# Recurrent attention with two expert mixtures: the old state added on TensorE, and y taken to rows and logits in f32

## The chip, the core and the metric

The kernel runs on one core of a Trainium2 chip. The metric is the device time of one execution in microseconds (us). Engines: PE is TensorE, DVE is VectorE, ACT is ScalarE, POOL is GpSimd, SP issues most of the DMAs.

## The reference, cut to what matters

Four batches of eight heads, 768 steps, head width 48. A recurrence makes y; its rows, 384 wide, go through two mixtures of eight experts, each row to one expert at most in each mixture.

```python
for t in range(S):
    state = alpha[:, :, t, :, None] * state + np.einsum('bhd,bhe->bhde', k[:, :, t], v[:, :, t])
    y[:, :, t] = np.einsum('bhd,bhde->bhe', q[:, :, t], state)
x = y.transpose(0, 2, 1, 3).reshape(B * S, H * D)
do_compute = x @ w_skip > 0                  # first mixture: other rows pass unchanged
e_idx = np.argmax(xc @ w_gate, axis=1)       # xc = x[do_compute]
y[mask] = gate_w[mask, None] * (np.maximum(xc[mask] @ w1[e], 0.0) @ w2[e])
...                                          # second mixture: all rows, its own gate and weights
```

## The kernel before, in words

**Attention by chunks.** The 768 steps of a batch are six chunks of 128, so there are 24 chunks (g) in all, c = 0 to 5 within a batch. Eight heads are four pairs, two heads of a pair on partitions 0 to 63 and 64 to 127. `prep` (L506) scans alpha's products over the chunk on DVE (L511, L515) and multiplies them into k and q, on GpSimd for most chunks (L519, L520). `emit_a` (L524) makes the scores (`ap`, L531), masks one half of the heads on DVE (L539) and the other on ACT and GpSimd (L536, L537), and transposes the keys (`kp`, L546). `emit_y` (L551) makes y in PSUM from the scores and from the old state (`yp`, L563 to L568). ACT writes 64 times y as f16 (`yh`, L571) and DVE the remainder as f16 (`yl`, L591). It then makes the chunk's own part of the state (`sp`, L578, L579); DVE adds the old state (L583) and multiplies by the chunk's whole decay (L585; L587 in the first chunk of a batch, which has no old state). `emit_r` (L602), one chunk late, turns y into rows and, in the same products, into the logits of both gates: the operand holds a selection of the pair's columns and the weights, in f16 halves (`rh`), so there are two products per pair, with `yh` (L612) and with `yl` (L613). ACT copies the rows out (L614), DVE sums the logits over the pairs and halves (L615).

**Order.** The order on every engine is the order of the code; nothing is reordered. An iteration g of the loop (L717) issues `emit_a(g+1)`, `prep(g+3)`, `emit_y(g)`, `emit_r(g-1)`. Between them `rt` puts short steps of the routing (`softmax_pick`, `rank`, `index`, `order`), which are mostly on DVE, some on PE (L284, L347); three chunks are one group of the routing. From g = 6 on, every second iteration splits a quarter of the first expert's weights into halves (`split_w`, L172: ACT, then GpSimd or DVE, L180).

**PSUM.** Banks have tags. `kp` and both `rp` (the rows' products) of a chunk share tag K with two banks, in turn; so the transposes of a chunk's keys wait until an earlier chunk's logits have been summed (L615). `ap`, `yp` and `sp` share tag B with four banks.

**Behind the attention.** The first mixture's tiles (gathered rows) and then the second's run as long rows of f16 products on PE, with weights streamed in by SP. They wait at their start for the last rows and lists of the routing.

Of the kernel before, what the change touches and what calls it, by code (L numbers as in the profile page):

```python
# [20 lines left out]
C = 128  # L21
# [9 lines left out]
# Each mixture's experts in the order of work: expert 0 first, in two parts (the second part's rows come from the last  # L31
# rows to be routed), then the others by falling length of their lists.
# [17 lines left out]
# further steps of routing in a chunk's time  # L50
RT = [1, 1, 1, 1, 1, 1, 1, 1, 1, 1, 1, 1, 1, 1, 1, 1, 0, 2, 0, 2, 10, 10, 7, 14]
# where the second mixture's first tiles are turned
TURNS2 = ((0, 3), (1, 1), (1, 5), (2, 1))
REL3 = (2, 1, 3, 3, 3, 3, 3, 1, 1)
# the chunks from which on GpSimd masks all scores
MASKP = 22
# steps of routing, and the ticks that a turn on TensorE waits, in the first mixture's parts
# [10 lines left out]
# in the second mixture's first part and in the others: where the weights are split, and the next part's tiles turned  # L68
SPLITS2 = (((2, 0), (2, 2), (2, 4), (2, 6)), ((0, 3), (0, 6), (1, 3), (1, 6)))
TURNS = (((2, 1), (2, 3), (2, 5)), ((0, 1), (1, 1), (2, 1), (2, 4)))  # L70
# quarters of an expert's weights whose lower halves GpSimd makes
# [35 lines left out]
def body(tc, qka, vN, rw, wg2, wg17, w1a, w2a, w1b, w2b, cst, zr, out, stop=9, dbg=None):  # L107
# [3 lines left out]
    with ctx:  # L111
# [15 lines left out]
        # sums of the logits in halves of the heads, scaled by SX twice  # L127
        lg = const.tile([128, 2, NB, 17], F32, name="lg")
        # selection of a head pair's rows, and the upper and lower halves of the scaled weights for the logits
        rh = const.tile([YP, NP, 130], F16, name="rh")  # L130
        wg2s = const.tile([128, 3, 8], F32, name="wg2s")
        # identity, and the halves of the second gate's scaled weights
# [5 lines left out]
        with ExitStack() as fctx, tc.manual_schedule():  # L138
# [6 lines left out]
            def bank(tag, name, *shape, parts=128, bufs=2):  # L145
                """a bank of PSUM, its front as [parts, *shape]"""
                t = ps.tile([128, 512], F32, tag=tag, name=name, bufs=4 if tag == "B" else bufs)
                v = t[0:parts, 0:int(np.prod(shape))]
                if len(shape) == 2:
                    v = v.rearrange("p (a b) -> p a b", a=shape[0])  # L150
                elif len(shape) == 3:
                    v = v.rearrange("p (a b c) -> p a b c", a=shape[0], b=shape[1])
                return v
# [41 lines left out]
            # Its short dependent steps are generators: 0 is yielded after each, 1 before TensorE's turn, 2 while it  # L195
            # waits for another, and the phases spread them between their own instructions.
# [31 lines left out]
            def finish(*which):  # L228
                """runs the given generators to their ends"""
                while any(r in active for r in which):  # L230
                    release()
                    rt()

            def softmax_pick(l, n, w, res, scale=1.0):
                """l: [128, n, w, 8]; gives the first maximum's one-hot and the exponentials of the scaled logits"""
# [29 lines left out]
            # running counts of the lists' entries in each partition  # L265
# [7 lines left out]
            def hold():  # L273
                """the bank of the short products, for one generator at a time, and TensorE's turn"""
# [5 lines left out]
            def rank(n, nl, ohm, before, res):  # L280
                """places of the rows in their lists, after those counted in before"""
# [11 lines left out]
            def wait(what, i):  # L293
                """until as many groups of rows are counted or indexed"""
# [9 lines left out]
            def numbered(n, nl, ohm, b0):  # L304
                """the one-hots times the two parts of the rows' numbers, 8 * blk + (partition + 1)"""
# [5 lines left out]
            def index(i, n, nl, ohm, on, rk, cols, region, first, last):  # L311
                """adds the rows' numbers to idx_ps at their places"""
# [48 lines left out]
            def order(i, counts):  # L361
                """the lists by falling length, the first list first: one-hot places of the lists [place, list]; each
                list's room; the order of the weights"""
# [33 lines left out]
            def ordered(i, src, t, dst):  # L397
                """dst [128, 7, t]: the index columns of the lists but the first in their order"""
# [14 lines left out]
            def to_lhs(x, hi, lo, m, tag="K"):  # L413
                """x: [m, 384] rows -> hi, lo: [128, 3, m]"""
# [6 lines left out]
            def ffn1(x, n, nf, xs, hs, each):  # L421
                """relu(x @ w1) as two halves hs: [128, 8, n]"""
# [16 lines left out]
            def ffn2(x, yp, hs, c, each):  # L439
                """h @ w2 for the rows c of h"""  # L440
# [7 lines left out]
            def ffn2t(x, c0, c1, hs, yps, each):  # L448
                """(h @ w2) transposed for the rows c0 to c1 of h: yps of [128, rows], in thirds of the columns"""
# [19 lines left out]
            def turn1(j, t):  # L469
                """a tile's rows as the columns of a product's operand"""  # L470
# [35 lines left out]
            def prep(g, parts):  # L506
                """products of alpha over the chunk's prefixes into q, their inverses into k"""
# [16 lines left out]
            def emit_a(g):  # L524
                """decayed scores of a chunk, keys by queries, masked; the keys transposed"""
# [25 lines left out]
            def emit_y(g):  # L551
                """y of a chunk from its scores and the state; the state's step"""
# [3 lines left out]
                yh, yl = st["ys", g] = [wk.tile([YP, NP, C], F16, tag=f"y{h}", name=f"y{h}") for h in "hl"]  # L556
                # the last chunk's in two banks, each read while the other is filled
                n = 2 if g == NB - 1 else NP
                for p0 in range(0, NP, n):
# [11 lines left out]
                    A.activation(out=yh[:, p0:p0 + n], in_=yp, func=AF.Copy, scale=SX)  # L571
                    if n < NP:
                        V.scalar_tensor_tensor(out=yl[:, p0:p0 + n], in0=yp, scalar=SX, in1=yh[:, p0:p0 + n], op0=ALU.mult, op1=ALU.subtract)
                if c < NC - 1:
                    ks = st.pop(("ks", g))
                    sp = bank("B", "sp", NP, D)
                    for p in range(NP):
                        T.matmul(sp[0:64, p, :], lhsT=ks[:, p, 0:64], rhs=v[:, p, 0:48], start=True, stop=True)  # L578
                        T.matmul(sp[64:128, p, :], lhsT=ks[:, p, 64:128], rhs=v[:, p, 48:96], start=True, stop=True)  # L579
                    sn = wk.tile([GP, NP, D], F32, tag="s", name="s")  # L580
                    e = pt.pop(g)[:, :, C:C + 1].to_broadcast([GP, NP, D])
                    if c:
                        V.tensor_tensor(sn, st.pop(("s", g)), sp, op=ALU.add)  # L583
                        rt()
                        V.tensor_tensor(sn, sn, e, op=ALU.mult)  # L585
                    else:
                        V.tensor_tensor(sn, sp, e, op=ALU.mult)  # L587
                    st["s", g + 1] = sn
                    rt()
                if n == NP:  # L590
                    V.scalar_tensor_tensor(out=yl, in0=yp, scalar=SX, in1=yh, op0=ALU.mult, op1=ALU.subtract)  # L591
                else:
                    release()
# [8 lines left out]
            def emit_r(g):  # L602
                """rows of x and their logits of both gates"""
# [3 lines left out]
                yh, yl = st.pop(("ys", g))  # L607
                for i2 in range(2):
                    rp = bank("B" if g == NB - 1 else "K", "rp", 2, 130)
                    for p in range(2):  # L610
                        q = 2 * i2 + p
                        T.matmul(rp[:, p, :], lhsT=yh[:, q, :], rhs=rh[:, q, :], start=True, stop=False)  # L612
                        T.matmul(rp[:, p, 0:113], lhsT=yl[:, q, :], rhs=rh[:, q, 0:113], start=False, stop=True)  # L613
# [581 lines left out]
```

## Time and profile before

| | us |
|---|---|
| median of 3 runs | 627.39 (622.05 to 632.94) |
| profiled execution, span from first to last instruction | 635.2 |
| PE busy | 538.6 (85%) |
| DVE busy | 430.5 (68%) |
| ACT busy | 252.5 (40%) |
| POOL busy | 315.5 (50%) |

The profile gives the span of its execution and no other time for it. A busy share is a mean over stages: the first 200 us are the attention, the rest the mixtures. "Idle before" names what ended an engine's wait. The chain of waits is followed back from the last instruction, at each step to what released it or to the instruction before it on its engine. The granted clock is a share of TensorE's full speed. A product in f32 shows as two records on PE.

### The profile page before, as it was taken

How to read it: one execution, taken by the hardware profiler on the slowest of the kernel's cores; microseconds unless marked ns; L12 is line 12 of the kernel's file. 1: busy time of each engine (PE TensorE's matmuls, PEld its weight loads, DVE VectorE, ACT ScalarE, POOL GpSimd, SP SyncE). 2: the span in 40 equal slices, each digit the busy share in tenths (PEclk: the TensorE clock that was granted, in tenths of full speed). 3: DMA queues.
4: the chain of work that ended last, by engine and by line, in shares of the span. 5: the costliest groups of instructions: out<-in, count | busy, mean ns of one | idle time of the engine just before them, and what ended most of it. 6: DMA issues, size and time to landing. Idle time of an engine off the chain costs nothing.

```text
span 635.2 us, 12933 instructions
## 1 busy us (share of the span) xinstructions
PE 538.6 (85%) x5089; PEld 385.7 (61%) x5089; DVE 430.5 (68%) x1123; ACT 252.5 (40%) x483; POOL 315.5 (50%) x269
## 2 busy tenths in 40 slices
PE   7898687697699779998868897979797989898994
PEld 4665454464467668888757866636364656564662
DVE  7988998989969788989889892381251626252530
ACT  2232332333334345555435623443353535443430
POOL 2453534434524575666655507366355555655501
PEclk7696996968869999999879998989898999998998
DMA  9561760653313765766665318435253344362001
GB/s 313 179 245 57 269 225 18 211 170 120 114 53 97 244 193 191 244 210 195 219 184 191 103 43 284 152 90 199 103 158 124 119 159 152 124 199 75 33 2 35
DMA packets 41464, 96.81 MB, mean 152 GB/s; under 512 B 3638, under 2 KB 28468, under 8 KB 41398
## 3 DMA queue, kind: packets, MB, share of 16 engines
q1 hardware_dynamic: 36662, 82.40, 38.9%
q0 software_dynamic: 4736, 13.53, 6.9%
q8 instruction: 42, 0.69, 0.5%
q14 instruction: 24, 0.20, 0.1%
HBM read 83.43 MB, written 12.99 MB: 152 GB/s over the span
## 4 chain that ended last, share of the span: by engine, by line
PE 48%; DVE 34%; issue 9%; another core or an unknown queue 3%; ACT 3%; DMA 2%; POOL 0%; POOLq 0%; DVEq 0%; ACTq 0%; SPq 0%
PE hp L431 6%; PE hp L432 6%; PE hp L430 6%; PE yp L443 4%; PE yp L444 4%; PE yp L445 4%; PE yp L567 3%; DVE pp L511 3%; DVE qka L515 3%; PE yp L563 2%; DVE s L585 2%; PE tp L417 2%; DVE hl L436 1%; DVE yl L591 1%
## 5 line engine op out<-in xcount | busy, mean ns | idle before, releaser
L436 DVE SCALAR_TENSOR_TENSOR h2l<-hp,h2h 128x352 f16<-128x352 f32 (+8 forms) x66 | 38.3, 586 | 105.4 <-ACT h2h L435 104.0
L180 POOL TENSOR_TENSOR w1l<-raw,w1h 128x768 bf16<-128x768 f32 x47 | 76.6, 1649 | 56.2 <-ACT w1h L178 56.0
L180 POOL TENSOR_TENSOR w0l<-raw,w0h 128x768 bf16<-128x768 f32 x47 | 77.3, 1651 | 45.9 <-ACT w0h L178 45.6
L519 POOL TENSOR_TENSOR qka<-qka 128x512 f32<-128x512 f32 (+1 forms) x24 | 27.5, 1147 | 91.1 <-DVE qka L515 72.0
L431 PE MATMUL hp<-x2l,w0h 128*128 128x352 f16 (+8 forms) x216 | 70.6, 331 | 1.4 <-DVE x2l L419 1.4
L430 PE MATMUL hp<-x2h,w0h 128*128 128x352 f16 (+8 forms) x216 | 71.0, 333 | 0.0
L432 PE MATMUL hp<-x2h,w0l 128*128 128x352 f16 (+8 forms) x216 | 70.5, 331 | 0.0
L443 PE MATMUL yp<-w1h,h2h 128*128 128x384 f16 (+1 forms) x192 | 63.2, 329 | 3.8 <-DVE h2l L436 3.8
L956 POOL DMA_INDIRECT out<-o,ixo x31 | 31.5, 1017 | 66.4 <-ACT o L1032 46.9
L431 PE MATMUL hp<-xl,w0h 128*128 128x200 f16 (+7 forms) x216 | 55.6, 265 | 10.4 <-DVE xl L419 10.2
L444 PE MATMUL yp<-w1l,h2h 128*128 128x384 bf16 (+1 forms) x192 | 63.2, 329 | 0.0
L445 PE MATMUL yp<-w1h,h2l 128*128 128x384 f16 (+1 forms) x192 | 63.1, 329 | 0.0
L432 PEld LDWEIGHTS <-w0l 128*128 128x128 bf16 x432 | 44.2, 102 | 29.3 <-POOL w1l L180 10.8
L455 PE MATMUL yp<-hl,w1h 128*128 128x200 f16 (+7 forms) x216 | 52.6, 252 | 3.9 <-DVE hl L436 3.9
L430 PE MATMUL hp<-xh,w0h 128*128 128x200 f16 (+7 forms) x216 | 55.8, 266 | 0.2 <-ACT xh L418 0.2
L432 PE MATMUL hp<-xh,w0l 128*128 128x200 f16 (+7 forms) x216 | 55.7, 266 | 0.0
L178 ACT ACTIVATE w0h<-raw 128x768 f16<-128x768 f32 x64 | 53.4, 836 | 3.7 <-DMA raw<-in_w1a 2.2
L454 PE MATMUL yp<-hh,w1h 128*128 128x200 f16 (+7 forms) x216 | 52.8, 252 | 2.5 <-ACT hh L435 2.4
L178 ACT ACTIVATE w1h<-raw 128x768 f16<-128x768 f32 x64 | 51.5, 836 | 6.6 <-DMA raw<-in_w2b 5.7
L435 ACT ACTIVATE h2h<-hp 128x352 f16<-128x352 f32 (+8 forms) x66 | 33.8, 513 | 50.5 <-PE hp L432 47.4
L431 PEld LDWEIGHTS <-w0h 128*128 128x128 f16 x432 | 44.4, 103 | 15.5 <-issue 1.5
L430 PEld LDWEIGHTS <-w0h 128*128 128x128 f16 x432 | 44.4, 103 | 15.2 <-issue 1.4
(185 smaller groups left out, 1495.0 us busy)
## 6 DMA issues: line engine op xcount, KB each, us to landing
qka<-in_qka SPq DMA_DIRECT2D x21, 772.0 KB
raw<-in_w1a SPq DMA_DIRECT2D x8, 1536.0 KB
raw<-in_w2a SPq DMA_DIRECT2D x8, 1536.0 KB
raw<-in_w1b SPq DMA_DIRECT2D x8, 1536.0 KB
raw<-in_w2b SPq DMA_DIRECT2D x8, 1536.0 KB
xrows<-xr SPq DMA_DIRECT2D x8, 591.0 KB
v<-in_vN SPq DMA_DIRECT2D x24, 192.0 KB
xrows<-x SPq DMA_DIRECT2D x9, 197.0 KB
```

What stands on the lines that cost most here:

```text
L178: A.activation(out=hi[:, sl], in_=r[:, sl], func=AF.Copy)
L180: eng.tensor_tensor(lo[:, sl], r[:, sl], hi[:, sl], op=ALU.subtract)
L430: T.matmul(hp[:, i], lhsT=wh[:, k, f], rhs=xh[:, k, 0:n], start=(k == 0), stop=False)
L431: T.matmul(hp[:, i], lhsT=wh[:, k, f], rhs=xl[:, k, 0:n], start=False, stop=False)
L432: T.matmul(hp[:, i], lhsT=wl[:, k, f], rhs=xh[:, k, 0:n], start=False, stop=(k == 2))
L435: A.activation(out=hh[:, f0:f0 + nf, 0:n], in_=hp, func=AF.Relu)
L436: V.scalar_tensor_tensor(out=hl[:, f0:f0 + nf, 0:n], in0=hp, scalar=0.0, in1=hh[:, f0:f0 + nf, 0:n], op0=ALU.max, op1=ALU.subtract)
L443: T.matmul(yp, lhsT=hs[0][:, f, c], rhs=wh[:, f], start=(f == 0), stop=False)
L444: T.matmul(yp, lhsT=hs[0][:, f, c], rhs=wl[:, f], start=False, stop=False)
L445: T.matmul(yp, lhsT=hs[1][:, f, c], rhs=wh[:, f], start=False, stop=(f == 7))
L454: T.matmul(yp, lhsT=wh[:, f, ds], rhs=hs[0][:, f, c0:c1], start=(f == 0), stop=False)
L455: T.matmul(yp, lhsT=wh[:, f, ds], rhs=hs[1][:, f, c0:c1], start=False, stop=False)
```

## The change

The state: the old state enters the same accumulation in PSUM as the chunk's own part, as a product with the identity in f32, and one multiply by the decay, which reads PSUM, remains on DVE. y: ACT copies it to SBUF as f32, without the factor 64, and nothing else reads it from PSUM. Rows and logits: one f32 product per pair with the f32 operand `rws`, which was loaded before too; its halves `rh` are no longer made. The logits are no longer scaled by 64 twice, so the softmax needs no scale. Comments are removed elsewhere; the diff is cut to the code.

```diff
-        rh = const.tile([YP, NP, 130], F16, name="rh")
...
             def emit_y(g):
-                yh, yl = st["ys", g] = [wk.tile([YP, NP, C], F16, tag=f"y{h}", name=f"y{h}") for h in "hl"]
+                y = st["ys", g] = wk.tile([YP, NP, C], F32, tag="y", name="y")
...
-                    A.activation(out=yh[:, p0:p0 + n], in_=yp, func=AF.Copy, scale=SX)
-                    if n < NP:
-                        V.scalar_tensor_tensor(out=yl[:, p0:p0 + n], in0=yp, scalar=SX, in1=yh[:, p0:p0 + n], op0=ALU.mult, op1=ALU.subtract)
+                    A.activation(out=y[:, p0:p0 + n], in_=yp, func=AF.Copy)
                 if c < NC - 1:
                     ks = st.pop(("ks", g))
                     sp = bank("B", "sp", NP, D)
+                    if c:
+                        T.matmul(sp, lhsT=ident, rhs=st.pop(("s", g)), start=True, stop=False)
                     for p in range(NP):
-                        T.matmul(sp[0:64, p, :], lhsT=ks[:, p, 0:64], rhs=v[:, p, 0:48], start=True, stop=True)
-                        T.matmul(sp[64:128, p, :], lhsT=ks[:, p, 64:128], rhs=v[:, p, 48:96], start=True, stop=True)
+                        T.matmul(sp[0:64, p, :], lhsT=ks[:, p, 0:64], rhs=v[:, p, 0:48], start=(c == 0), stop=(c == 0 or p == NP - 1))
+                        T.matmul(sp[64:128, p, :], lhsT=ks[:, p, 64:128], rhs=v[:, p, 48:96], start=(c == 0), stop=(c == 0 or p == NP - 1))
                     sn = wk.tile([GP, NP, D], F32, tag="s", name="s")
-                    e = pt.pop(g)[:, :, C:C + 1].to_broadcast([GP, NP, D])
-                    if c:
-                        V.tensor_tensor(sn, st.pop(("s", g)), sp, op=ALU.add)
-                        rt()
-                        V.tensor_tensor(sn, sn, e, op=ALU.mult)
-                    else:
-                        V.tensor_tensor(sn, sp, e, op=ALU.mult)
+                    V.tensor_tensor(sn, sp, pt.pop(g)[:, :, C:C + 1].to_broadcast([GP, NP, D]), op=ALU.mult)
                     st["s", g + 1] = sn
-                    rt()
-                if n == NP:
-                    V.scalar_tensor_tensor(out=yl, in0=yp, scalar=SX, in1=yh, op0=ALU.mult, op1=ALU.subtract)
-                else:
+                    rt(2)
+                if n < NP:
                     release()
...
             def emit_r(g):
-                yh, yl = st.pop(("ys", g))
+                y = st.pop(("ys", g))
                 for i2 in range(2):
-                    rp = bank("B" if g == NB - 1 else "K", "rp", 2, 130)
+                    rp = bank("B" if g == NB - 1 else "K", "rp", 2, 113)
                     for p in range(2):
                         q = 2 * i2 + p
-                        T.matmul(rp[:, p, :], lhsT=yh[:, q, :], rhs=rh[:, q, :], start=True, stop=False)
-                        T.matmul(rp[:, p, 0:113], lhsT=yl[:, q, :], rhs=rh[:, q, 0:113], start=False, stop=True)
-                    A.activation(out=xr[i][:, k, i2 * 192:(i2 + 1) * 192].rearrange("p (a b) -> p a b", a=2), in_=rp[:, :, 0:96], func=AF.Copy, scale=1 / SX)
-                    V.tensor_reduce(lg[:, i2, g, :], rp[:, :, 96:130].rearrange("p a (t b) -> p b a t", t=2), axis=AX.XY, op=ALU.add)
+                        T.matmul(rp[:, p, :], lhsT=y[:, q, :], rhs=rws[:, q, :], start=True, stop=True)
+                    A.activation(out=xr[i][:, k, i2 * 192:(i2 + 1) * 192].rearrange("p (a b) -> p a b", a=2), in_=rp[:, :, 0:96], func=AF.Copy)
+                    V.tensor_reduce(lg[:, i2, g, :], rp[:, :, 96:113].rearrange("p a b -> p b a"), axis=AX.X, op=ALU.add)
...
-                yield from softmax_pick(l[:, :, 1:17].rearrange("p a (w e) -> p a w e", w=2), n, 2, res, SX ** -2)
+                yield from softmax_pick(l[:, :, 1:17].rearrange("p a (w e) -> p a w e", w=2), n, 2, res)
...
-                    V.tensor_scalar(x[:, :, LOG:], l[:, :, 9:17], SX ** -2, None, op0=ALU.mult)
+                    V.tensor_copy(x[:, :, LOG:], l[:, :, 9:17])
...
-            P.tensor_copy(rh[:, :, 0:96], rws[:, :, 0:96])
-            halves_of(rws[:, :, 96:], rh[:, :, 96:113], rh[:, :, 113:])
```

## Rows read from the trace of the kernel before

**Rows 1.** Windows of the attention: window, length, busy us per engine, granted clock, DMA.

```profile
20.00:200.00 180.00, 150.03 (x1660) 98.46 (x1657) 161.06 (x438) 59.08 (x132) 78.69 (x76) 0.82 0.42 144
...
98.60:102.00 3.40, 0.70 (x6) 0.58 (x6) 3.33 (x8) 0.00 (x0) 2.73 (x3) 0.78 0.00 0
102.00:105.40 3.40, 3.40 (x24) 1.65 (x22) 3.37 (x12) 0.60 (x1) 0.00 (x0) 0.50 0.02 5
105.40:108.80 3.40, 3.40 (x27) 1.89 (x24) 1.19 (x3) 1.09 (x3) 2.32 (x2) 0.50 0.00 0
```

**Rows 2.** The chain that ended last, 20 to 200 us: shares by line.

```profile
by line: PE yp L567 11.6%; DVE pp L511 9.2%; PE yp L563 8.2%; DVE qka L515 7.3%; DVE s L585 6.9%; DVE yl L591 5.2%; PE ap L531 4.5%; PE kp L546 4.5%; PE yp L564 4.1%; issue 4.0%; DVE eq L251 3.4%; PE sp L578 2.8%; DVE at L539 2.7%; DVE mv L
```

**Rows 3.** The same chain in order of time: start us, us, what.

```profile
27.44 0.27 PE sp L578
...
28.47 0.22 PE rp L612
...
49.63 1.28 DVE s L585
...
97.96 1.29 DVE s L585
...
99.24 1.56 DVE ohm L633
...
100.80 0.60 DVE yl L591
...
148.78 1.28 DVE s L585
...
180.93 0.22 PE rp L612
...
188.44 0.19 PE sp L578
```

**Rows 4.** DVE by line: count, busy us, mean ns (L587: its min/median/max).

```profile
L585 DVE TENSOR_TENSOR s<-s,pp 128x192 f32<-128x192 f32 x16 | 14.7, 916 | 0.2
...
L583 DVE TENSOR_TENSOR s<-s,sp 128x192 f32<-128x192 f32 x16 | 5.5, 347 | 10.2 <-PE sp L579 10.2
...
L591 DVE SCALAR_TENSOR_TENSOR yl<-yp,yh 112x512 f16<-112x512 f32 x23 | 15.6, 680 | 4.5 <-ACT yh L571 4.5
...
L587 DVE TENSOR_TENSOR s<-sp,pp x4: 331/331/331, 22.1 to 164.0; 128x192 f32<-128x192 f32 x4
```

**Rows 5.** GpSimd in order of time: start us, us, what.

```profile
96.72 1.18 POOL L519 TENSOR_TENSOR qka<-qka 128x512 f32<-128x512 f32 x1 [3.06 <-DVE qka L515]
97.86 1.17 POOL L520 TENSOR_TENSOR qka<-qka,pp 128x512 f32<-128x512 f32 x1
98.98 1.75 POOL L180 TENSOR_TENSOR w0l<-raw,w0h 128x768 bf16<-128x768 f32 x1
```

**Rows 6.** Two lines of DVE: count, ns min/median/max, first and last start.

```profile
L511 DVE TENSOR_TENSOR_SCAN pp<-qka,bz x24: 1197/1226/2700, 4.0 to 176.6; 128x520 f32<-128x520 f32 x24
...
L633 DVE TENSOR_TENSOR ohm<-eq,cm x7: 193/629/1634, 50.8 to 192.9; 128x48 f16<-128x48 f32 x7
```

**Rows 7.** PE in order of time, and all records of L563.

```profile
63.01 0.27 PE L564 MATMUL yp<-at,v 128*48 128x128 f32 x1
...
63.12 0.27 PE L564 MATMUL yp<-at,v 128*48 128x128 f32 x1
...
81.95 0.23 PE L612 MATMUL rp<-rh,yh 112*128 112x130 f16 x1
...
82.34 0.21 PE L613 MATMUL rp<-rh,yl 112*128 112x113 f16 x1
...
L563 PE MATMUL yp<-at,v x192: 272/323/476, 15.4 to 197.7; 128*64 128x128 f32 x192
```

**Rows 8.** Waits, 20 to 200 us: us in total, times, longest.

```profile
PE rk L284 <- DVE ohm L633: 15.9, 5, 4.0
...
PE kp L546 <- DVE lg L615: 9.2, 11, 2.3
```

## The prediction

> **What bounds the kernel now.** The change touches only the attention, the first 200 us of the span of 635.2; the mixtures behind it run on code that it leaves alone, so what is won or lost there is carried to the end. I read the windows first. The reader should see in them that no single engine bounds this stage: over 20 to 200 us DVE is busy 161.1 us of 180 and PE 150.0, at a mean granted clock of 0.82 [rows 1]. The three short windows show how the two take turns. From 98.6 to 102 DVE is full and PE does 0.7 us of work in 3.4; then the clock falls to 0.50, the lower of its two levels (1.2 of 2.4 GHz), and from 102 to 108.8 PE is full while DVE does 4.6 of 6.8 us.
>
> The chain of waits says the same in order of time. It passes from DVE to PE and back, and of 180 us it has 6.9% on the decay of the state (L585) and 5.2% on the lower halves of y (L591) [rows 2]; both go with the change. A stretch of it [rows 3] shows why PE waits for them: L585, the routing's L633, then L591 stand in DVE's queue ahead of the logits' sum, L615, and the transposes of the next chunk's keys (L546) need the bank of PSUM that this sum reads [rows 8].
>
> **What goes from DVE.** The add (L583, 16 times 347 ns) and the decay (L585, 916 ns in the mean) become one multiply that reads PSUM; its form is already there for the first chunks, L587, 331 ns all four times [rows 4]. It takes the add's place on the chain at the add's price. L591 goes outright, 23 times 680 ns (and its two halves in the last chunk). Off DVE's queue go 16 x 0.916 + 16 x 0.347 - 16 x 0.331 + 15.6 = 30.5 us; off the chain, by its shares, 6.9% + 5.2% of 180 us = 21.8 us. I take the second.
>
> **What of this comes back.** L585 is long because of GpSimd. It reads two tensors of SBUF; at 97.96 it ends when L520, which GpSimd began at 97.86, is over (99.03), and L633 behind it, of the same kind, ends after the split L180 that began at 98.98 [rows 3, 5]. The multiply that reads PSUM doesn't wait. But the wait passes on: without L585, L633 meets L520 in its place. The scan L511, too, took up to 2.70 us where its median is 1.23 [rows 6]. The lower bound is no return, the upper the whole excess, 16 x (0.916 - 0.331) = 9.4 us. Five L585 of about 1.28 us stand on the chain, from 49.63 to 148.78, with an L633 behind them, which at 97.96 is the longer one and elsewhere takes 0.6 us, its median [rows 3, 6]: in four of them the change saves the 0.6, not the 1.28, and 0.7 us returns each time, 2.8 us. With a little for the scans I take 3.4 us, nearer to the lower end, since the other eleven decays have no such step behind them.
>
> The Trainium skill (SBUF — State Buffer, the section on the ports) states that the pair of ports that VectorE shares with GpSimd is locked for a whole instruction, by VectorE instructions with two SBUF inputs too, and that the loser blocks. By that rule the removed wait goes to the next such instruction in full, as the third rival below has it; the trace agrees on who waits, and leaves open how much returns.
>
> **What PE gets.** The rows and logits: eight f16 products start between 81.95 and 82.34 and need 0.44 us with the last; afterwards there are four in f32, each in two passes, as the records show it for the 96 products of L563 (192 records) [rows 7]. One pass of 128 columns starts 0.11 us after the one before (63.01 to 63.12) [rows 7]. Eight passes of 113 columns are 0.75 us if the columns decide and 0.88 if the weights of 128 do; I take 0.88, the row that is nearest (128 full weights), thus 0.44 more per chunk. The state's product with the identity is two passes of 192 columns, 0.33 us, in 16 chunks. That is 24 x 0.44 + 16 x 0.33 = 16 us at full clock, 32 at half. Much of it lies under DVE's stretches. On the chain the rows' products stand in four places, from 28.47 to 180.93, all at half clock, and the state's products in seven, from 27.44 to 188.44, three of them at half clock [rows 3]: 4 x 0.88 + 4 x 0.33 + 3 x 0.66 = 6.8 us. Where PE waits for the logits' sum only about 0.8 us each time (9.2 in 11) [rows 8], PE's added work uses up the gap, and I count 1 us lost there.
>
> **What the clock gives.** Five times PE waited some 3 us for L633 (15.9 us in all, the longest 4.0) [rows 8], and after the one at 98 us the clock fell. These waits shrink from both sides: L633 comes about 0.6 to 1.6 us earlier and PE has 0.8 us more to do before it; 1 to 2 us are left, between those that led to a fall and the 0.8 that didn't. I count three of the five half-clock spells behind these waits gone. One such spell leaves DVE 2.2 us idle (102 to 108.8: 4.56 of 6.80 busy) [rows 1], which is what can come forward; so 3 x 2.2 = 6.6 us. Bounds: none, and five, 11 us.
>
> **Edits at nothing.** ACT's copies of y and of the rows keep their sizes, and ACT is busy 59 of 180 us [rows 1]. The logits' sums read half as much, 48 times, in place. The halves of the selection matrix at the start go from ACT, DVE and GpSimd; they stand before the first chunk, beside the first scans, once. Two routing steps now follow the multiply together; they are as many as before except one more in each batch's first chunk. The product with the identity waits for the old state, but the products of y just before it wait for that already. No DMA is added or moved past another on SP's or POOL's queue. The last chunk loses L573 and gains 0.44 us on PE, about even.
>
> **Sum:** -21.8 + 3.4 + 6.8 + 1.0 - 6.6 = -17.2 us. The profile gives one time, the span of 635.2 us, 7.8 over the runs' median of 627.39; the difference goes to the median: 610 us, or 618 for a span like the profiled one.
>
> **Rivals.**
> First, **PE becomes the bound** and no half-clock spell goes: the gain is 21.8 - 3.4 - 6.8 - 1.0, less 2 to 5 us in chunks where PE, now about 0.8 us longer, has no gap left: about 7 us, 620 us. For it speaks that PE already works 150 of 180 us [rows 1]; against it, that nearly half of these are at half clock only because DVE let it wait.
> Second, on the other side, **the f32 products at half clock**: if the spells last as long in work as before and the stage runs on PE's queue from end to end, nearly all of the 32 us lie on the chain, and of DVE's 21.8 at most 15 count, since DVE then waits: 17 us slower, 644 us. It decides once PE is full at a granted clock below about 0.6 over the stage, against 0.82 now. Against it: at half clock DVE is idle only about a third of the time [rows 1], so less than half of the stage is PE's.
> Third, **the wait stays with DVE**: all of the 9.4 us return to L633, the routing's other sums and the scans. Then -21.8 + 9.4 + 6.8 + 1.0 and one spell, -2.2, give 7 us: 620 us. L511's longest speaks for it [rows 6], the short routing steps without GpSimd beside them against it.
> That the change doesn't do what it says is hardly open: the instructions are there or not.
>
> **How the numbers follow.** Forecast 0.56, first rival 0.24, third 0.13, second 0.07. Two per cent (12.5 us) is about what a measurement of this kernel can tell from no change; its three runs spread over 10.9 us. The forecast lies mostly beyond 2%, with a part within; rivals one and three lie within, and second mostly beyond on the slow side: faster 0.56, same 0.38, slower 0.06. The range's lower end takes no return and all five spells (-21.8 + 6.8 - 11 = -26, 601 us) and 2 us of the runs' spread, 599 us; the upper end takes the first and third rivals with 4 us for the runs' spread: 624 us. The forecast's own range is 600 to 616.
>
> **What would show it.** Right: L587's form 20 times at about 0.33 us, no L591; L633 or a scan grown by part of what L585 lost; rows' products 0.88 us a chunk at full clock; the wait for L633 below 2 us; fewer slices below 10 in the clock's line; the last product of L563 near 181 us in place of 197.7 [rows 7]. Wrong: DVE's waits moved in full (the two-input steps' mean near 1 us more), PE's share above 95% with the clock where it was, or the mixtures' stretch longer than before.

## The result, and the profile after

On the first comparison the changed kernel took 609.31 us (median of 4 runs, 603.83 to 611.11) against 626.08 (4 runs, 622.05 to 632.94): ratio 0.971, 95% interval 0.966 to 0.976. Two later comparisons, on chips that the table below names 7 and 14, gave 0.971 (0.966 to 0.976) and 0.977 (0.972 to 0.981). That is 15 to 18 us less. The ratios are taken over undisturbed executions alone, so a ratio times the median of before can differ from the difference of two medians (on chip 14 14.8 us by the ratio, 17.2 by the medians). The forecast was 17.2 us less, but two terms of its sum, of opposite sign, came out far from their sizes, and a part of the gain lies behind the attention, where the forecast had none.

**The stage.** The last product of yp starts at 179.2 us of the span instead of 197.7 [rows 7]. First the windows of the changed kernel (window, length, busy us per engine, granted clock, DMA): the stage from its first to its last product of yp, the window of [rows 1], and three short ones around a place where GpSimd multiplies.

```profile
15.40:180.00 164.60, 149.50 (x1707) 105.44 (x1704) 154.19 (x396) 61.09 (x129) 79.58 (x77) 0.96 0.47 164
20.00:200.00 180.00, 161.39 (x1836) 116.59 (x1835) 164.82 (x463) 68.10 (x144) 86.30 (x85) 0.97 0.48 167
88.60:92.00 3.40, 2.37 (x30) 2.06 (x29) 3.37 (x8) 1.99 (x4) 3.06 (x3) 1.00 0.03 7
92.00:95.40 3.40, 3.40 (x38) 1.92 (x37) 3.30 (x8) 0.90 (x2) 1.44 (x2) 1.00 0.00 0
95.40:98.80 3.40, 2.80 (x34) 2.33 (x35) 3.40 (x13) 1.87 (x5) 1.21 (x2) 1.00 0.00 0
```

The same stage of the kernel before, which is longer:

```profile
15.40:198.50 183.10, 152.45 (x1677) 100.84 (x1677) 164.28 (x437) 58.80 (x129) 80.60 (x78) 0.81 0.43 147
```

The stage is 18.5 us shorter: DVE is busy 10.1 us less (164.28 to 154.19) and idle 8.4 us less (18.8 to 10.4). PE got more to do and is busy 3.0 us less, because the granted clock is 0.96 instead of 0.81. In [rows 1] a full DVE left PE with 0.7 us of work in 3.4; at such a place PE now has 2.37, and the clock stays at 1.00.

**What PE waits for**, 20 to 200 us (total, times, longest), beside [rows 8]:

```profile
PE idx_ps L345 <- DVE hot L340: 6.7, 4, 2.3
PE rk L282 <- DVE ohm L622: 4.9, 5, 1.3
PE kp L544 <- DVE lg L604: 3.1, 5, 0.9
```

15.9 us of waits for the routing's masked picks (L633, now L622) became 4.9, and the longest 4.0 became 1.3. The waits for the logits' sum fell from 9.2 to 3.1 us. A wait for another step of the routing (`hot`, now L340) grew; in the kernel before it was

```profile
PE idx_ps L347 <- DVE hot L342: 2.2, 2, 1.8
```

so the three together fell from 27.3 to 14.7 us.

**DVE by line**, 20 to 200 us (count, busy us, mean ns), after and then before. The lines are moved up: L579 is the multiply, L622 was L633, L639 was L650 (a copy now, a multiply by a constant before), L637 L648, L297 L299, L613 L624.

```profile
L579 DVE TENSOR_TENSOR s<-sp,pp 128x192 f32<-128x192 f32 x20 | 6.9, 345 | 3.6 <-PE sp L577 3.6
L622 DVE TENSOR_TENSOR ohm<-eq,cm 128x48 f16<-128x48 f32 x8 | 6.9, 868 | 0.2
L639 DVE COPY xr<-lg 128x24 f32<-128x24 f32 x8 | 5.7, 719 | 0.0
L637 DVE TENSOR_TENSOR xr<-den 128x3 f32<-128x3 f32 x8 | 5.6, 697 | 0.0
L297 DVE TENSOR_TENSOR cum<-cum,ohm 128x16 f16<-128x16 f16 x8 | 4.9, 614 | 0.1
L613 DVE TENSOR_TENSOR lg<-lg 128x51 f32<-128x51 f32 x8 | 4.3, 536 | 0.4 <-DVE rg L678 0.2
```

```profile
L633 DVE TENSOR_TENSOR ohm<-eq,cm 128x48 f16<-128x48 f32 x7 | 4.6, 651 | 0.0
L650 DVE TENSOR_SCALAR xr<-lg 128x24 f32<-128x24 f32 x7 | 1.2, 165 | 0.0
L648 DVE TENSOR_TENSOR xr<-den 128x3 f32<-128x3 f32 x7 | 2.3, 328 | 0.0
L299 DVE TENSOR_TENSOR cum<-cum,ohm 128x16 f16<-128x16 f16 x7 | 2.3, 331 | 0.1
L624 DVE TENSOR_TENSOR lg<-lg 128x51 f32<-128x51 f32 x7 | 2.2, 321 | 0.2
```

The multiply is as forecast, 20 times 345 ns. But small steps, of 3 to 51 elements in a row, now take up to 0.87 us in the mean. For L639 the new instruction isn't the reason: as a multiply it takes 720 ns in the state's part alone on chip 15, and as a copy 167 ns in y's part alone (both kernels are described below). What makes them long is seen where GpSimd (first fence, as in [rows 5]) and the chain's DVE pieces (second fence: start, us, what) are laid side by side:

```profile
88.94 1.18 POOL L517 TENSOR_TENSOR qka<-qka 128x512 f32<-128x512 f32 x1 [2.67 <-DVE mx L247]
90.08 1.17 POOL L518 TENSOR_TENSOR qka<-qka,pp 128x512 f32<-128x512 f32 x1
91.21 1.65 POOL L178 TENSOR_TENSOR w0l<-raw,w0h 128x768 bf16<-128x768 f32 x1
```

```profile
88.95 0.27 DVE s L579
89.21 0.99 DVE eq L249
90.20 0.02 issue
90.22 1.09 DVE ohm L622
91.32 0.20 DVE lg L604 x2
91.52 1.37 DVE cum L297
```

Each of the three GpSimd instructions has one DVE step that ends when it ends: L249 at 90.20 (L517 until 90.12), L622 at 91.31 (L518 until 91.25), L297 at 92.89 (L178 until 92.86). The multiply and the logits' sum, which read PSUM, run through at 0.27 and 2 x 0.10 us on the chain. So a wait for GpSimd isn't tied to L585: a GpSimd product mostly catches a step of DVE whose inputs lie in SBUF, whichever stands there. Of the stage's 47 such GpSimd instructions (L517, L518 and the splits L178) 36 end within 0.25 us of a DVE step of this kind that took over 0.3 us, and 28 and 32 in the two later executions; in the kernel before it was 25. Plain copies are caught too (L639, up to 1.16 us). The Trainium skill (SBUF — State Buffer, Who interferes with whom) lists copies among the operations that can contend with GpSimd for the ports that the two share, and this trace agrees.

**The clock, by product.** All records of the first product of yp (ns min/median/max, first and last start), beside [rows 7]: the median fell from 323 to 273 ns in this execution (to 276 on chip 14; on chip 7 it stayed at 323).

```profile
L561 PE MATMUL yp<-at,v x192: 272/273/477, 15.1 to 179.2; 128*64 128x128 f32 x192
```

**Behind the stage.** The second mixture's products (first and last start) in the two kernels, run beside each other on chip 7, before and after:

```profile
L443 PE MATMUL yp<-w1h,h2h x192: 322/326/527, 376.3 to 619.7; 128*128 128x384 f16 x184, 128*120 128x384 f16 x8
```

```profile
L441 PE MATMUL yp<-w1h,h2h x192: 323/326/527, 362.0 to 598.7; 128*128 128x384 f16 x184, 128*120 128x384 f16 x8
```

It starts 14.3 us earlier, and takes 236.7 instead of 243.4 us though its code is the same. So of the 21.1 us between these two spans (629.8 and 608.7) the stage has 11.5, and 9.6 arise behind it. In the first pair of profiles it starts 20.4 us earlier and is 7.3 us shorter (240.4 to 247.7), so that the two spans there differ by 27.6 us and the medians by 16.8: the profiled execution of before was a long one (its span of 635.2 is above the longest of the four runs, 632.94).

### The profile page after: what moved, and what is told of

Its sections match the earlier page's. It is cut to its first block, busy times and chain, and to the rows that moved or that the text cites. A ratio compares the mean times of both kernels' runs of the same rounds, so it can differ in the third digit from the quotient of the medians.

```text
span 607.6 us, 12952 instructions
## 1 busy us (share of the span) xinstructions
PE 533.8 (88%) x5121; PEld 389.2 (64%) x5121; DVE 419.4 (69%) x1081; ACT 254.7 (42%) x482; POOL 314.0 (52%) x268
## 4 chain that ended last, share of the span: by engine, by line
PE 42%; DVE 41%; issue 8%; ACT 3%; another core or an unknown queue 2%; DMA 1%; POOL 0%; POOLq 0%; DVEq 0%; ACTq 0%
PE hp L429 6%; PE hp L430 6%; PE hp L428 6%; DVE pp L509 5%; PE yp L441 5%; PE yp L443 5%; PE yp L442 5%; DVE qka L513 4%; PE tp L415 2%; DVE hl L434 2%; DVE at L537 2%; DVE cum L300 1%; DVE w1l L178 1%; DVE ohm L824 1%
## 5 line engine op out<-in xcount | busy, mean ns | idle before, releaser
L178 POOL TENSOR_TENSOR w1l<-raw,w1h 128x768 bf16<-128x768 f32 x47 | 77.5, 1666 | 52.4 <-ACT w1h L176 52.3
L178 POOL TENSOR_TENSOR w0l<-raw,w0h 128x768 bf16<-128x768 f32 x47 | 77.2, 1651 | 40.6 <-ACT w0h L176 40.2
L517 POOL TENSOR_TENSOR qka<-qka 128x512 f32<-128x512 f32 (+1 forms) x24 | 27.5, 1146 | 82.7 <-DVE qka L513 62.7
L429 PE MATMUL hp<-xl,w0h 128*128 128x200 f16 (+7 forms) x216 | 54.0, 260 | 7.8 <-DVE xl L417 7.6
L430 PEld LDWEIGHTS <-w0l 128*128 128x128 bf16 x432 | 43.3, 100 | 26.1 <-POOL w1l L178 8.5
L428 PE MATMUL hp<-xh,w0h 128*128 128x200 f16 (+7 forms) x216 | 54.1, 260 | 0.0
L430 PE MATMUL hp<-xh,w0l 128*128 128x200 f16 (+7 forms) x216 | 54.0, 260 | 0.0
L454 PE MATMUL yp<-hh,w1l 128*128 128x200 f16 (+7 forms) x216 | 53.5, 255 | 0.0
L428 PEld LDWEIGHTS <-w0h 128*128 128x128 f16 x432 | 43.3, 100 | 14.8 <-issue 0.8
```

Source lines behind the costliest of these rows:

```text
L178: eng.tensor_tensor(lo[:, sl], r[:, sl], hi[:, sl], op=ALU.subtract)
L428: T.matmul(hp[:, i], lhsT=wh[:, k, f], rhs=xh[:, k, 0:n], start=(k == 0), stop=False)
L429: T.matmul(hp[:, i], lhsT=wh[:, k, f], rhs=xl[:, k, 0:n], start=False, stop=False)
L430: T.matmul(hp[:, i], lhsT=wl[:, k, f], rhs=xh[:, k, 0:n], start=False, stop=(k == 2))
L454: T.matmul(yp, lhsT=wl[:, f, ds], rhs=hs[0][:, f, c0:c1], start=False, stop=(f == 7))
```

## The experiments

Three theories of the result were put against each other. **The chain's sum**: what left DVE's queue on the chain is the gain, less a wait that returns. **The wait comes back**: DVE's waits for GpSimd go over to the next steps, and the gain comes from PE's waits and clock. **PE's work holds the clock**: more work on PE alone keeps its clock up. The texts written before the runs call the second theory D and the third C. The batches ran on three chips; every ratio is against the kernel before on the same chip, with its 95% interval. All in one table: the last start of yp's first product; the stage from 15.4 us to 0.8 us behind it; PE's waits for the masked picks (20 to 200 us). The columns from the last start on are of one profiled execution each; that of e2b_y was one of its three longest (633.93 us), that of e8_before_steps its shortest.

| kernel | chip | us, median | ratio | last start | clock | DVE busy + idle | PE busy | PE's waits |
|---|---|---|---|---|---|---|---|---|
| r_before | 7 | 628.12 | 0.998 (0.994 to 1.001) | 197.7 | 0.80 | 162.6 + 20.5 | 150.6 | 16.6 |
| r_after | 7 | 610.02 | 0.971 (0.966 to 0.976) | 186.2 | 0.93 | 149.9 + 21.7 | 154.5 | 5.5 |
| e4_y16 | 7 | 607.38 | 0.966 (0.961 to 0.970) | 180.6 | 0.86 | 149.8 + 16.2 | 145.5 | 9.9 |
| e7_steps | 7 | 602.66 | 0.958 (0.955 to 0.962) | 175.8 | 0.98 | 150.0 + 11.2 | 148.0 | 4.0 |
| e1_state | 15 | 602.38 | 0.997 (0.992 to 1.001) | 186.5 | 0.88 | 157.6 + 14.3 | 148.0 | 3.0 |
| e2_y | 15 | 605.44 | 1.000 (0.996 to 1.004) | 197.4 | 0.83 | 152.4 + 30.4 | 161.5 | 13.2 |
| e5_before_pe | 15 | 609.73 | 1.008 (1.003 to 1.012) | 200.3 | 0.83 | 162.9 + 22.7 | 160.6 | 13.5 |
| e6_k_dve | 15 | 611.14 | 1.009 (1.005 to 1.014) | 197.8 | 0.86 | 158.8 + 24.3 | 165.1 | 3.2 |
| r2_after | 14 | 613.66 | 0.977 (0.972 to 0.981) | 182.8 | 0.93 | 150.9 + 17.3 | 152.4 | 4.5 |
| e1b_state | 14 | 621.68 | 0.987 (0.983 to 0.991) | 194.3 | 0.81 | 153.6 + 26.1 | 160.1 | 6.4 |
| e2b_y | 14 | 630.63 | 1.000 (0.995 to 1.004) | 199.9 | 0.81 | 151.5 + 33.8 | 163.6 | 13.1 |
| e8_before_steps | 14 | 620.40 | 0.989 (0.985 to 0.993) | 180.7 | 0.88 | 159.7 + 6.4 | 141.4 | 7.5 |

**The state's part alone** (the kernel before with the identity product and one multiply; y stays in f16 halves), on two chips:

```diff
+                    if c:
+                        T.matmul(sp, lhsT=ident, rhs=st.pop(("s", g)), start=True, stop=False)
...
-                        V.tensor_tensor(sn, st.pop(("s", g)), sp, op=ALU.add)
-                        rt()
-                        V.tensor_tensor(sn, sn, e, op=ALU.mult)
+                    V.tensor_tensor(sn, sp, pt.pop(g)[:, :, C:C + 1].to_broadcast([GP, NP, D]), op=ALU.mult)
```

> The kernel before with the state's part of the change alone: the old state enters as a product with the identity, one multiply from PSUM is left on DVE; y still goes as two f16 halves. Theory D (DVE's queue bounds the attention; the half-clock spells of PE are what DVE's queue makes PE wait for): 14.6 us go from DVE's queue (16 x 0.35 + 16 x 0.92 - 16 x 0.35), about half of it returns as waits for GpSimd at other steps, and one or two half-clock spells go: 8 to 12 us faster than before, 614 to 618 us, granted clock over the attention 0.85 to 0.92. Theory C (the added f32 work on PE keeps the clock up, and that is the gain): only 16 x 0.33 us are added to PE, so the clock stays near 0.82 and the gain is 4 us or less, 622 us or more.

> The state part alone, a second time, beside the whole change. By shares of the chain of before it should give 6.9% of 180 us less 1.3 for the two products and less a part that returns, some 5 to 8 us (0.988 to 0.992); it gave 0.9965 before, with the clock at 0.88 and last yp product at 186.5. 'The parts do not add': 0.985 to 1.0, clock between the kernel before and the changed one. 'They add': this and the y part together give the whole, thus 0.98 to 0.985.

Measured: 0.997 and 0.987, that is 2 us (no change within its interval) and 8 us, at clocks of 0.88 and 0.81: neither theory's gain and clock came out together in either run.

**y's part alone** (the changed kernel with DVE's add and decay restored, the reverse of that diff):

> The changed kernel with the state's part undone (DVE adds the old state and multiplies, no product with the identity); y goes as f32 to rows and logits. Theory D: 15.6 us go from DVE's queue (L591 of before), less comes back than with the state's part, since L585 still takes its place beside GpSimd's products: 9 to 13 us faster than before, 613 to 617 us, clock 0.88 to 0.95. Theory C: two thirds of the added PE work are here (24 x 0.44 us), so nearly the whole gain stands, 609 to 613 us, clock 0.95 or more.

> The y part alone, a second time, beside the whole change. By shares of the chain 5.2% of 180 us less 3.5 for the f32 products is 6 us (0.990); it gave 1.0001 before, with the last yp product where the kernel before has it (197.4). 'The parts do not add': 0.99 to 1.005, clock near 0.82 in 20 to 180 us. 'They add': 0.985 to 0.99.

Measured: 1.000 both times, although 16 us of L591 left DVE's queue. Both theories had expected a gain of 9 us or more at a clock of 0.88 or more; it was 0.83 and 0.81.

The whole change beside both on chip 14, and with the kernel before on chip 7:

> The changed kernel once more, beside its two parts on the same chip. On two comparisons it was 0.971 of the kernel before, with the last start of the yp product at 179.2 and 186.2 us of the span (197.7 in the kernel before). 'The chip decides': if the chip on which the parts were first run takes the gain away, this run gives 0.99 or more there, with half-clock spells left in the attention. 'The parts do not add': about 0.97 wherever it runs, clock of 20 to 180 us above 0.92, while the two parts beside it stay above 0.985 each.

> The changed kernel itself beside the experiments. If the change gives on this chip what it gave in the first comparison, 0.971 times the time before, 588 us. If its gain was mostly the half-clock spells and these are fewer here, the DVE time that it frees (10 us in the first pair of traces) is what remains, 596 to 600 us. From the two parts run alone (602.4 and 605.4 us) added up: 602 us.

> The kernel before itself, for a trace on the same chip as the experiments, where its median is 606 us and not 626. If the chips differ in the mixtures alone, the attention is as in the first trace (last product of L563 near 198 us, granted clock 0.82) and the mixtures are some 20 us shorter. If the attention differs, fewer half-clock spells stand in it (clock 0.88 or more) and its last product is near 185 us.

r_after and r_before were expected on the chip of the first parts, with its 606 us, but ran on chip 7; so of their texts only the ratio can be held against the result, and it is 0.971 again. On chip 14 the parts give 8 + 0 us and the whole 14.8 (0.977 of 630.83): the parts don't add, and it isn't the chip. Where a part's saving went shows in DVE's idle time ahead of single lines (last column, with what ended it), 20 to 200 us, y's part alone on chip 15:

```profile
L608 DVE TENSOR_REDUCE lg<-rp 128x17 f32<-128x34 f32 x46 | 7.5, 186 | 12.7 <-ACT xr L607 12.7
L579 DVE TENSOR_TENSOR s<-s,sp 128x192 f32<-128x192 f32 x16 | 5.5, 346 | 13.2 <-PE sp L575 13.2
```

and the state's part alone on chip 14:

```profile
L583 DVE TENSOR_TENSOR s<-sp,pp 128x192 f32<-128x192 f32 x20 | 7.0, 349 | 17.5 <-PE sp L581 17.4
```

In the kernel before DVE waited 10.2 us for PE ahead of the state's step [rows 4]; either part alone can make that 13 to 17 us (the state's part had 9.3 in its execution on chip 15, where the stage ended earlier, at 186.5; the whole change has 3.6, 9.0 and 7.2 in its three), and y's part adds 12.7 us ahead of the logits' sum, which waits for ACT, and ACT for the rows' products. PE is then busy 160 to 164 us of the stage at a clock of 0.81 to 0.83, as slow as before. That comes near the forecast's first rival, PE as the bound, above all in y's part alone, although PE still waits 13 us for the picks there. The state's part alone makes the waits for the picks short, too (3.0 and 6.4 us), but PE then still waits for the logits' sum, which stands behind the lower halves of y on DVE as before; on chip 14:

```profile
PE kp L546 <- DVE lg L611: 8.3, 10, 1.9
PE rk L284 <- DVE ohm L629: 6.4, 4, 2.2
```

The waits for picks, logits' sum and `hot` together take 27 to 28 us of the stage in the kernel before, 17 and 20 with the state's part, 19 and 20 with y's, and 14 to 15 with both. With both the clock is 0.93 to 0.96 in three executions; with one part it was above 0.83 once, at 0.88.

**More work on PE, nothing else** (the kernel before, with the rows' f16 products issued twice):

```diff
-                    for p in range(2):
+                    for p in (0, 1, 0, 1):
```

> The kernel before with the f16 products of rows and logits issued twice into the same bank: 24 x 0.44 us more on PE, as much as the change adds there for the rows, and nothing on DVE. Theory D: the half-clock spells stay (granted clock 0.80 to 0.85 over the attention) and the time is that of before or up to 6 us more, 625 to 632 us. Theory C: the clock rises to 0.90 or more and the time falls by 6 us or more, to 620 us or less.

4.7 us slower, clock 0.83, PE's waits 13.5 us. More work on PE alone doesn't bring the clock up, and it gains no time; as the cause of the gain that theory falls.

**y as f16, with one f16 product** in the changed kernel; the lower halves of y and of the operand (`rws16`, made once at the start) are left out, so its rows and logits are less exact:

```diff
-                y = st["ys", g] = wk.tile([YP, NP, C], F32, tag="y", name="y")
+                y = st["ys", g] = wk.tile([YP, NP, C], F16, tag="y", name="y")
...
-                        T.matmul(rp[:, p, :], lhsT=y[:, q, :], rhs=rws[:, q, :], start=True, stop=True)
+                        T.matmul(rp[:, p, :], lhsT=y[:, q, :], rhs=rws16[:, q, :], start=True, stop=True)
```

> The changed kernel with y as f16 and one f16 product per pair for rows and logits (the lower halves are left out, and the operand is rounded to f16): 24 x 0.66 us less on PE, nothing changed on DVE. If DVE alone bounds the attention, the time of the changed kernel within 3 us. If PE's f32 products now lie on the path, 5 to 10 us faster than the changed kernel. If they kept the clock up, more half-clock spells and 3 us or more slower.

2.6 us less than the change beside it, with four runs each and intervals that overlap: near the forecast's 3.5 for these products, and not clear of nothing. The clock fell, from 0.93 to 0.86, and PE's waits for the picks rose from 5.5 to 9.9 us, since PE has less to do before each. So in the changed kernel the f32 products do help to keep the clock up, but the time doesn't hang on it: the stage ends at 180.6, within the 179.2 to 186.2 of the change.

**k's product on DVE** in the changed kernel (GpSimd keeps q's):

```diff
-            whole, halves = ((slice(0, NP), P, P),), ((slice(0, 2), V, V), (slice(2, NP), P, V))
+            whole, halves = ((slice(0, NP), V, P),), ((slice(0, 2), V, V), (slice(2, NP), P, V))
```

> The changed kernel with k's product (L517) on DVE in place of GpSimd in 21 chunks: 21 x 0.69 = 14.5 us more work on DVE, 21 x 1.18 us less on GpSimd. If DVE's two-input steps wait for GpSimd's products by about 20 us in all, as the growth of the routing's steps in the changed kernel suggests, half of that goes with the product: 3 to 7 us slower than the changed kernel, 612 to 616 us, and the steps behind the scan (the one-hot, the copies into the rows) fall to 0.2 to 0.6 us. If that growth is no wait for GpSimd, all 14.5 us stand: 622 to 626 us and the steps stay as long as they are.

0.9% slower than the kernel before. The changed kernel wasn't run on this chip; by its 0.971 elsewhere it would take some 588 us here, an estimate, so that this edit costs some 23 us, more than either reading expected. Half of GpSimd's products are gone from DVE's way, but DVE pays 16.8 us for them (22 times 764 ns; one of these was there before) and the other half finds other steps (the comparisons of L340 took 657 ns in the mean). It takes more than it gives; it doesn't measure the wait alone.

**The order of the routing's steps.** In the changed kernel the two steps behind the multiply go ahead of the second scan, so that they run while GpSimd has nothing to multiply:

```diff
                 V.reciprocal(bz2.rearrange("p (a c) -> p a c", a=NP)[:, :, C + 1:], pp[:, :, C:C + 1])
-                rt()
+                rt(1 if g < 3 or (g - 3) % NC == NC - 1 else 3)
...
-                    rt(2)
+                    rt(0 if g + 3 < NB else 2)
```

> The changed kernel with the two routing steps behind the state's multiply moved ahead of the second scan (L513), where GpSimd mostly waits for that scan; the same instructions otherwise. If the wait for GpSimd came back at these steps (some 20 us in all on DVE in the changed kernel's trace), a third to a half of it goes: 5 to 9 us faster than the changed kernel. If the wait only moves on to the steps behind emit_r and to the mask, within 2 us of it.

602.66 us, 7.4 less than the change beside it, and at 0.958 the best ratio of all kernels run. The same order in the kernel before (its steps behind the add and behind the decay):

> The kernel before with only the order of e7_steps: the routing steps that stand behind the add and behind the decay of the state go ahead of prep's second scan, in the chunks that still have a prep. It tells whether the 7 us that this order gave the changed kernel belong to the order or to the change. 'The wait returned there': with L585 still in place to take GpSimd's wait itself, moving the short steps gains less, 0 to 3 us (0.995 to 1.0). 'The order is better anyway' (the routing's sums come earlier and PE waits less for them): 6 to 8 us here too (0.987 to 0.990), with PE's waits for L633 (15.9 us in 20 to 200) below 8.

0.989, 7 us less: the order is worth as much without the change, so e7 by itself doesn't show that a returned wait was taken away. What it shows is which step must stay out of GpSimd's way. The kernel before in this order, GpSimd's and DVE's instructions side by side as start, us, what:

```profile
90.59 1.18 POOL L519 TENSOR_TENSOR qka<-qka 128x512 f32<-128x512 f32 x1 [3.55 <-DVE qka L515]
91.73 1.29 POOL L520 TENSOR_TENSOR qka<-qka,pp 128x512 f32<-128x512 f32 x1
```

```profile
90.42 0.18 DVE L633 TENSOR_TENSOR ohm<-eq,cm 128x48 f16<-128x48 f32 x1
90.52 0.35 DVE L583 TENSOR_TENSOR s<-s,sp 128x192 f32<-128x192 f32 x1
90.90 1.08 DVE L585 TENSOR_TENSOR s<-s,pp 128x192 f32<-128x192 f32 x1
```

L633 stands ahead of GpSimd's L519 and takes 0.18 us instead of 1.56 [rows 3]; L585 behind it still waits until L519 is over (91.98 and 91.77). PE's waits for L633 fall from 16 to 7.5 us in all:

```profile
PE rk L284 <- DVE ohm L633: 7.5, 5, 1.9
```

and the stage ends 17 us earlier with 159.7 us of work left on DVE, in that profiled execution, which was the shortest of its six (614.26; the median is 620.40). The changed kernel in the new order, DVE again:

```profile
87.73 0.18 DVE L622 TENSOR_TENSOR ohm<-eq,cm 128x48 f16<-128x48 f32 x1
...
89.18 1.06 DVE L297 TENSOR_TENSOR cum<-cum,ohm 128x16 f16<-128x16 f16 x1
90.16 0.19 DVE L316 TENSOR_REDUCE r<-ad 128x3 f32<-128x48 f32 x1
90.27 1.56 DVE L300 TENSOR_TENSOR cum<-cum,ohm 128x16 f16<-128x16 f16 x1
```

Here too L622 is short, and the waits sit in L297 and L300 behind it: they end at 90.24 and 91.83, and GpSimd's L518 and L178 at 90.21 and 91.82. DVE's busy time is the same 150.0 us as in r_after: the waits were moved, not removed, to steps that PE needs later.

## Why the prediction was right, point by point

**What goes from DVE: as counted.** 16.0 (L591 and its halves) + 14.7 + 5.5 - (6.9 - 1.3) = 30.6 us left its queue; 30.5 were forecast. That 21.8 of it counts on the chain wasn't a property of the lines: y's share of it, 5.2% of 180 us, gave nothing alone, since DVE then waited for PE; beside the state's part it gave 6.6 us (0.987 less 0.977, of 630.83; the two intervals nearly touch).

**What comes back: the term that was mis-sized.** Forecast 3.4 us, at most 9.4. By the sums of all lines DVE's work in the stage fell by 13.3 us (189.8 to 176.5), and by 16.8 on chip 7 (188.3 to 171.5), where 30.6 and 31.6 were removed: 17 and 15 us came back. The records of neighbouring steps overlap, so the lines' sums are larger than the busy time, which fell by 10.1 and by 12.6 us (162.6 to 149.9). The bound failed because it took the excess of L585 as all that GpSimd could cost. In the kernel before L585 stood beside GpSimd's two-input instructions for 12.2 us of the 57 that these take, and L591 and L583, which read PSUM and don't wait, for another 10.4 (overlaps of the timeline's records); without them short steps of SBUF operands stand there and wait. In the stage the seven of each grew by 4.4 us in L639, 3.1 in L637, 2.5 in L297, 2.1 in L622 and 1.9 in L613, together 14.0 of the 17. So DVE's net saving was 10 to 13 us of busy time, where the forecast had 18.4 on the chain and, off the queue, 30.5 less 3.4 or 27.1. The third rival had this mechanism and too low a price for it; its time, 620 us, was not reached because its other terms changed too.

**What PE gets: right in kind, a little low.** The rows' eight passes fill 1.08 us to the next product at full clock (0.88 was taken), the identity's two 0.49 us (0.33). The row that the forecast took for 128 full weights, L564, loads only 48 columns of them (123 ns in the median); the rows' loads of 128 columns take 192 ns, the identity's 189. The starts in the changed kernel:

```profile
74.54 1.15 PE L602 MATMUL rp<-rws,y 112*128 112x113 f32 x8
75.62 0.60 PE L529 MATMUL ap<-qka 64*128 64x128 f32 x6
...
80.86 0.56 PE L574 MATMUL sp<-s,cs 128*128 128x192 f32 x2
81.35 0.26 PE L576 MATMUL sp<-v,ks 128*64 128x48 f32 x1
```

e4 (2.6 us, not clear of the noise) and e5 (4.7 us, for a load of f16 products) are near the 3.5 that the rows have in the forecast's 6.8. The identity's share of 3.3 wasn't measured by itself.

**What the clock gives: more than counted.** Three of five spells, 6.6 us, were taken. The waits for L633 fell by 11 us, while those for `hot` rose by 4 to 5, which the forecast left out. The longest for L633 fell as forecast to below 2 us in the first profile (1.3), and to 2.3 in the two later ones; the clock rose by 0.12 to 0.15, and PE did its larger work in 149.5 to 154.5 us against 150.6 to 152.5. Against the forecast of +6.8 + 1.0 - 6.6 = +1.2 us for all that isn't DVE's work, DVE's idle time changed by -8.4, on chip 7 by +1.1, and on chip 14, against the first profile of before, by -1.5 us. So in the first profile the clock made up for the returned wait; on chip 7 the stage won 11.5 us only.

**The rest of the time.** The stage gave 18.5, 11.5 and 14.9 us, the medians 16.8, 18.1 and 17.2 (14.8 by the ratio). The second mixture, whose code is the same, was 7 us shorter in the profiles of the change in the first comparison and on chip 7 (the records above). On chip 7 PE is idle 3.3 us less in it (17.3 for 20.6) and busy 3.4 us less, at a clock of 0.98 for 0.97; what sets this off isn't known. That part of the gain isn't explained, and the forecast, which took the mixtures as unchanged, had it at nothing. An earlier start isn't the reason: e8 starts it at 358.8 us, as early as the change does, and needs 243.7. It stays open.

**The other signs.** L587's form 20 times: yes. No L591: yes. A wait below 2 us for L633: in one of three. The last product near 181: 179.2, 186.2, 182.8. Fewer slices of the clock's line below its top digit: 3 of the first 13 instead of 8, in the first pair of profiles. DVE's short steps grew by 0.2 to 0.6 us in the mean, not by the 1 us that would have spoken against the forecast. The second rival, f32 products at half clock, was excluded: it needed PE full at a clock below 0.6, and the stage had 0.93 to 0.96, with PE busy 3.0 us less to 3.9 us more. So the way of the gain was seen rightly: DVE's queue gets shorter, PE waits less, and the clock rises. That the total came out within 1 us of 17.2 by the medians is partly luck: a returned wait of four to five times its forecast met a clock that gave more than counted and a mixture that got shorter for an unknown reason.

## What to carry to other kernels

Where GpSimd works on SBUF beside DVE, count what the removed DVE work had been standing beside: here instructions that read PSUM ran through GpSimd's (the multiply in 345 ns), and when they went, short SBUF steps took their place and waited until its instruction was over. A share of a chain that passes between two engines is no price for one edit: make sure that the other engine isn't the next bound, since either half alone gave 0 to 8 us here and both 15. Before work is removed, try the order: putting the one step that PE waits for ahead of GpSimd's products gave 7 us with or without the change.

## What the runs showed of the hardware

The length of the stage isn't a property of the code alone: the changed kernel's stage ended at 179.2, 182.8 and 186.2 us in three profiled executions, the state's part's at 186.5 and 194.3, with clocks of 0.96, 0.93, 0.93 and of 0.88, 0.81. The second mixture took 221 to 224 us in all four kernels run on chip 15 and 236 to 248 in all the others, with the same code: the kernel before had a median of 605.83 us there, of 629.16 on chip 7 and of 630.83 on chip 14. A difference of 4% between chips is larger than the effect studied, so times were compared only between kernels that ran beside each other.
